# Scores of whole query rows for a pair of heads, moved from one 128x128 matmul form to four 64x64 quarters of the tensor engine

## The chip, the cores and the metric

The kernel runs on one core of one Trainium2 chip. The metric is device time in microseconds of one execution. A core has a matrix engine (TensorE, "PE" in the profile, with its weight loads "PEld"), a vector engine (VectorE, "DVE"), a scalar engine (ScalarE, "ACT"), a general engine (GpSimd, "POOL") and an engine that here only starts transfers ("SP").

## The reference

Block sparse attention in fp32, then two dense layers with a squared ReLU:

```python
batch, n_heads, seq, head_dim = (4, 8, 768, 64)   # blocks of 32 rows, 24 blocks
scores = scale * np.matmul(q, k.transpose(0, 1, 3, 2))
mask = np.abs(blk_i - blk_j) <= window            # window = 1
mask = mask | (blk_i == 0) | (blk_j == 0) | (blk_i == n_blocks - 1) | (blk_j == n_blocks - 1)
for qb in range(n_blocks):
    for kb in sampled_blocks[qb]:                 # 3 random blocks each
        mask[qb * block:(qb + 1) * block, kb * block:(kb + 1) * block] = True
scores = np.where(mask, scores, -1000000000.0)
scores = scores - np.max(scores, axis=-1, keepdims=True)
attn = np.exp(scores)
attn = attn / (np.sum(attn, axis=-1, keepdims=True) + 1e-09)
attn_out = np.matmul(attn, v)
...
x = attn_out.transpose(0, 2, 1, 3).reshape(B * S, H * D)     # 3072 x 512
h = np.maximum(x @ w_in, 0.0)                                # 512 -> 2048
return h * h @ w_out                                         # 2048 -> 512
```

The first and the last block of query rows look at all 768 keys. They are the "whole rows" of this case.

## The kernel before, in words

The 3072 rows are cut into 24 tiles of 128 (four batches of six), and these into eight chunks of three tiles. The dense layers run chunk by chunk: `turn` transposes a chunk's attention output (`xt`, `xh`, `xl`), `hidden` makes one of 16 pieces of the first layer (`ph`, 12 matmuls of 128x128 weights by 384 columns, in a rounded fp32 form as high and low parts), `project` adds a piece into the output (`po`, nine matmuls by 512 columns), and `split` makes the high and low parts of the weights (`wi`, `wo`; the low part is a subtraction on GpSimd). `gf`, `gh` and `gl` are the squared hidden values and their high and low parts.

Attention for a later chunk is cut into small steps and woven into the dense work of the chunk before by `Stream`: each unit is a generator that yields how many pieces of dense work pass before its next step (the table `LAG`). The order on each engine is therefore the order in which the program is written; each engine works through its list in that order and waits where an input is missing. There is a prologue without dense work, in which the attention of chunk 0 is made.

A unit of class `Half` is a tile's 128 query rows for four heads: scores `s` (matmuls of 64 rows of contraction by 32 query rows, in eight quarters of the array), maxima `m`, exponentials `p` or `pm`, and the product with the values `pv`.

A unit of class `Whole` is the first and last block of query rows for a pair of heads: 2 heads x 2 blocks x 32 = 128 rows. There are 16 of them: four batches by four pairs. Batch 0's run in the prologue, those of batches 1 to 3 are spread over some 48 us of dense work around the starts of chunks 1, 3 and 5. Its steps are `scores`, `maxima`, `exps`, `move` (copies on ScalarE and GpSimd into `pgm`), `turn_blocks` (a blockwise transpose on VectorE; in the prologue `turn` and `copies` with TensorE instead), `values` (`pvg`, 24 records for 12 matmuls of 128x64 weights) and `norm`. Scores and other results of TensorE share five PSUM banks by turns (`bank`).

`QG` holds the query rows of a unit as the stationary operand, 128 rows of contraction: 64 for the first head and 64 for the second. For a head's query columns the other head's 64 rows are zeros, written by the host:

```python
qg = np.zeros((B, 2, D, NPAIR, 2, 2, BLK), np.float32)
...
for e in range(2):
    qg[:, e, :, :, e] = q6[:, e]
```

`kn` holds the keys of two pairs, both heads of a pair on the two halves of the partitions. So one 128x128 matmul gives both heads' scores for 512 keys and a second for 256 keys; `load_whole` brings `QG` once a batch, 256 KB. The maxima are taken per row over both banks, and their larger one, times -SCALE, is the bias of the two exponentials.

Of the kernel before, what the change touches and what calls it, by code (L numbers as in the profile page):

```python
# [10 lines left out]
F32 = mybir.dt.float32  # L11
# [3 lines left out]
AF = mybir.ActivationFunctionType  # L15
ALU = mybir.AluOpType
AX = mybir.AxisListType.X
# [5 lines left out]
B, H, S, D = 4, 8, 768, 64  # L23
BLK = 32
NBLK = S // BLK
NRAND = 3
P = 128
NT = S // P
NJ = P // BLK
NPAIR = H // 2  # L30
# [4 lines left out]
SCALE = 0.125  # L35
# [61 lines left out]
def tile_block_sparse_attention_moe(ctx: ExitStack, tc, kd, knd, qd, qgd, vd, vnd, samp, const, wcat, out):  # L97
# [9 lines left out]
    nc = tc.nc  # L107
    wide = wcat.dtype != F32

    one = ctx.enter_context(tc.tile_pool(name="one", bufs=1))  # L110
    rot = ctx.enter_context(tc.tile_pool(name="rot", bufs=2, reuse_waits="tile"))
# [3 lines left out]
    def bank(name):  # L115
        return ps.tile([P, 512], F32, tag="s", name=name)
# [36 lines left out]
            )  # L153
        return idx

    QG = one.tile([P, NPAIR, P], F32, name="QG")
    V = {0: [one.tile([P, 2, NJ, HW // 2], F32, name=f"V{c}") for c in range(2)]}
    W1 = {f: one.tile([P, DM], F32, name=f"W1{f}") for f in SINGLE}
    KG = [one.tile([P, NJ, 2 + NRAND, NPAIR, BLK], F32, name=f"KG{i}") for i in range(2)]
# [8 lines left out]
    def load_whole(b, eng=nc.sync):  # L168

        eng.dma_start(QG.rearrange("p a b -> p (a b)"), qgd[b])  # L170

# [57 lines left out]
    def centre(qb):  # L229
        return min(max(qb, 1), NBLK - 2)  # L230
# [90 lines left out]
    class Half:  # L321
# [36 lines left out]
        def scores(self):  # L358
            b, t, u = self.b, self.t, self.u
            q, kg, kn = st["q", b, t], st["kg", b, t], st["kn", b, u]  # L360
            self.sb = [bank(f"s{self.name}_{e}") for e in range(2)]
            for i in range(2):
                pr = 2 * u + i
                for piece in range(2):
                    for g, j in enumerate(self.js):
                        c = centre(NJ * t + j)
                        for e in range(2):
                            r = slice(e * D, (e + 1) * D)
                            if piece == 0:
                                k, a, z = kn[r, c - 1 : c + 2, i, :], S_WIN, NSLOT  # L370
                            else:
                                k, a, z = kg[r, j, :, pr, :], 0, S_WIN
                            nc.tensor.matmul(  # L373
                                self.sb[e][g * BLK : (g + 1) * BLK, i * NSLOT + a : i * NSLOT + z],
                                q[r, j, pr, :],
                                k,
                                start=True,
                                stop=True,
                            )

        def maxima(self):
            m = self.m = rot.tile([P, 2, 2], F32, tag="m", name=f"m{self.name}", bufs=4)
            at = self.rows
            for e in range(2):
                nc.vector.tensor_reduce(  # L385
                    m[at, e], self.sb[e][at].rearrange("p (i c) -> p i c", i=2), axis=AX, op=ALU.max
                )
            self.p = rot.tile([P, 4, 2, NJ, BLK], F32, tag="p", name=f"p{self.name}", bufs=PBUFS)
            if not self.moved:
                nc.vector.tensor_scalar(m[at], m[at], -SCALE, None, op0=ALU.mult)  # L390
                return
            for e in range(2):
                nc.vector.tensor_tensor(  # L393
                    self.p[at, 2 * e : 2 * e + 2].rearrange("p h c a s -> p h (c a s)"),
                    self.sb[e][at].rearrange("p (i c) -> p i c", i=2),
                    m[at, e].unsqueeze(2).broadcast_to([at.stop, 2, NSLOT]),
                    op=ALU.subtract,
                )
# [29 lines left out]
        def exps(self):  # L428
            at = self.rows
            for e in range(2):  # L430
                for i in range(2):
                    nc.scalar.activation(  # L432
                        self.p[at, 2 * e + i].rearrange("p c a s -> p (c a s)"),
                        self.sb[e][at, i * NSLOT : (i + 1) * NSLOT],
                        AF.Exp,
                        scale=SCALE,
                        bias=self.m[at, e, i : i + 1],
                    )

        def turn(self, bank):  # L440
            pt = [bank(f"pt{self.name}_{e}") for e in range(2)]
            n = self.rows.stop
            for e in range(2):
                for i in range(2):
                    for c in range(2):
                        a = (2 * i + c) * P
                        nc.tensor.transpose(pt[e][:, a : a + n], self.p[:n, 2 * e + i, c], ident[:n, :n])
            return pt

        def copies(self, pt):  # L450
            self.pT = rot.tile([P, NJ, 4, 2, BLK], F32, tag="pT", name=f"pT{self.name}", bufs=2)
            n = len(self.js)
            for e in range(2):
                src = pt[e].rearrange("p (h j q) -> p h j q", h=4, j=NJ)[:, :, :n]
                dst = self.pT[:, :n, 2 * e : 2 * e + 2].rearrange("p j i c q -> p (i c) j q")
                if e == 0 or self.k < UC:
                    nc.scalar.copy(dst, src)  # L457
                else:
                    nc.vector.tensor_copy(dst, src)
# [63 lines left out]
    class Whole:  # L523


        n = (16 * BLK, 8 * BLK)

        def __init__(self, b, pr):
            self.b, self.pr = b, pr
# [24 lines left out]
            self.norm(po)  # L554

        def scores(self):
            b, pr = self.b, self.pr
            kn = st["kn", b, pr // 2]
            self.sg = [bank(f"g{self.name}_{i}") for i in range(2)]
            for i, n in enumerate(self.n):  # L560
                k0 = 16 * i
                nc.tensor.matmul(  # L562
                    self.sg[i][:, :n], QG[:, pr], kn[:, k0 : k0 + n // BLK, pr % 2, :], start=True, stop=True
                )

        def maxima(self):
            m = self.m = rot.tile([P, 2], F32, tag="mg", name=f"mg{self.name}", bufs=2)
            for i, n in enumerate(self.n):
                nc.vector.tensor_reduce(m[:, i : i + 1], self.sg[i][:, :n], axis=AX, op=ALU.max)
            nc.vector.tensor_tensor(m[:, 0:1], m[:, 0:1], m[:, 1:2], op=ALU.max)  # L570
            nc.vector.tensor_scalar(m[:, 0:1], m[:, 0:1], -SCALE, None, op0=ALU.mult)

        def exps(self):
            tag, bufs = ("w", WBUFS) if self.b > 0 else ("p", PBUFS)
            self.p = rot.tile([P, S], F32, tag=tag, name=f"pg{self.name}", bufs=bufs)
            for i, n in enumerate(self.n):
                at = slice(i * self.n[0], i * self.n[0] + n)
                nc.scalar.activation(self.p[:, at], self.sg[i][:, :n], AF.Exp, scale=SCALE, bias=self.m[:, 0:1])

        def move(self):  # L580

# [12 lines left out]

        def turn(self, bank):
            pt = [bank(f"ptg{self.name}_{i}") for i in range(2)]
            for i, n in enumerate(self.n):
                at = i * self.n[0]
                for a in range(0, n, P):
                    nc.tensor.transpose(pt[i][:, a : a + P], self.p[:, at + a : at + a + P], ident)  # L600
            return pt

        def copies(self, pt):
            self.pT = rot.tile([P, S], F32, tag="pT", name=f"pTg{self.name}", bufs=2)
            for i, n in enumerate(self.n):
                at = i * self.n[0]
                if i == 0:
                    nc.scalar.copy(self.pT[:, at : at + n], pt[i][:, :n])
                else:
                    nc.vector.tensor_copy(self.pT[:, at : at + n], pt[i][:, :n])  # L610

        def values(self, bank):
            b, pr = self.b, self.pr
            vn = st["vn", b, pr // 2]
            po = bank(f"pvg{self.name}")
            for kt in range(NT):
                for e in range(2):
                    h = pr % 2 * 2 + e
                    a = kt * P + e * D
                    nc.tensor.matmul(  # L620
                        po[e * D : (e + 1) * D, :VW],
                        self.pT[:, a : a + D],
                        vn[:, kt, h * VW : (h + 1) * VW],
                        start=(kt == 0),
                        stop=(kt == NT - 1),
                    )
            return po
# [270 lines left out]
    start = tc.tile_pool(name="start", bufs=1)  # L898
# [130 lines left out]
```

## Time and profile before

| | |
|---|---|
| time, median of 3 runs | 753.91 us (751.81 to 755.79) |
| span of the profiled execution | 752.7 us |
| around the span, against the median | 1.2 us |
| TensorE busy | 725.9 us, 96% |
| VectorE, ScalarE, GpSimd busy | 506.2, 518.8, 499.4 us |
| records of the whole rows' scores (L562) | 64, 16 units |

The profiled execution has no time of its own beside its span; the runs shown are others of the same kernel. Busy time of TensorE counts overlapping matmuls once. The profile shows a matmul's start as it was dispatched, and its end is modelled, so lengths of a group are read from the starts of what follows, not from its own busy time.

### The profile page before, as it was taken

The numbers are of one execution on the slowest core, as the hardware profiler recorded it, in microseconds if no ns is written. First come the engines' busy times: TensorE is split into PE (matmuls) and PEld (weight loads), VectorE is DVE, ScalarE is ACT, GpSimd is POOL, SyncE is SP. The second block draws the span as 40 slices with busy tenths as digits, with TensorE's granted clock in tenths as the row PEclk, the third lists the DMA queues.
The fourth block names the chain that finished last, engine by engine and source line by source line (L and its number), as shares of the span: only waits on it lengthen the run. The fifth ranks groups of instructions, "written<-read, shape, count | busy, mean of one in ns | idle before, by whom it ended". The sixth has DMA issues, their size and how long they took to land.

```text
span 752.7 us, 24232 instructions
## 1 busy us (share of the span) xinstructions
PE 725.9 (96%) x8936; PEld 606.6 (81%) x8936; DVE 506.2 (67%) x1036; ACT 518.8 (69%) x1145; POOL 499.4 (66%) x624
## 2 busy tenths in 40 slices
PE   5779999999999999999999999999999999999997
PEld 2566776678888888887888888888888888888986
DVE  5785876758785756677877675667878666555452
ACT  5986787888876875588786777478976776623222
POOL 6963644237786675757777567675776575777885
PEclk9989999999999999999999999999999999999999
DMA  8785889562533435533534435544344342101001
GB/s 276 222 237 141 234 246 348 144 163 62 145 83 97 136 83 176 150 96 97 139 90 102 131 85 166 152 101 129 89 119 108 82 130 57 34 1 43 1 1 42
DMA packets 85786, 92.95 MB, mean 123 GB/s; under 512 B 13539, under 2 KB 73060, under 8 KB 85668
## 3 DMA queue, kind: packets, MB, share of 16 engines
q1 hardware_dynamic: 79684, 68.42, 34.4%
q0 software_dynamic: 5696, 22.58, 9.1%
q8 instruction: 71, 1.16, 0.7%
q14 instruction: 47, 0.39, 0.2%
q10 hardware_dynamic: 288, 0.39, 0.1%
HBM read 85.05 MB, written 6.29 MB: 121 GB/s over the span
## 4 chain that ended last, share of the span: by engine, by line
PE 77%; ACT 12%; DVE 7%; issue 2%; DMA 1%; POOL 1%; ACTq 0%; DVEq 0%; POOLq 0%
PE ph L804 31%; PE po L842 29%; PE s L373 6%; PE pv L471 5%; PE po L832 2%; ACT p L432 2%; PE g L562 2%; PE pvg L620 1%; ACT pm L418 1%; DVE m L385 1%; ACT craw L726 1%; PE xt L789 1%; ACT V L217 1%; ACT r L808 1%; ACT pT L457 1%
## 5 line engine op out<-in xcount | busy, mean ns | idle before, releaser
L804 PE MATMUL ph<-xh,wi 128*128 128x384 f32 x832 | 237.8, 346 | 0.0
L418 ACT ACTIVATE pm<-p 32x256 f32<-32x256 f32 x528 | 219.2, 415 | 16.9 <-DVE p L393 9.4
L842 PE MATMUL po<-wo,gh 128*128 128x512 f32 x672 | 213.8, 399 | 0.0
L771 POOL TENSOR_TENSOR wi<-W,wi 128x512 fp32r<-128x512 f32 x104 | 143.0, 1375 | 73.3 <-DVE wi L770 37.6
L808 ACT ACTIVATE r<-ph 128x384 f32<-128x384 f32 x128 | 63.0, 492 | 172.5 <-PE ph L804 171.6
L771 POOL TENSOR_TENSOR wo<-WO,wo 128x512 fp32r<-128x512 f32 x112 | 146.2, 1305 | 50.0 <-DVE wo L770 44.2
L822 POOL TENSOR_TENSOR gl<-gf,gh 128x384 fp32r<-128x384 f32 x112 | 117.3, 1048 | 85.8 <-DVE gf L820 73.2
L804 PEld LDWEIGHTS ph<-xh,wi 128*128 128x128 f32 x832 | 150.3, 188 | 13.1 <-issue 7.2
L820 DVE SCALAR_TENSOR_TENSOR gf<-ph,r 128x384 f32<-128x384 f32 x112 | 62.3, 556 | 141.8 <-ACT r L808 129.2
L842 PEld LDWEIGHTS po<-wo,gh 128*128 128x128 f32 x672 | 123.5, 188 | 22.8 <-issue 2.8
L804 PE MATMUL ph<-xl,wi 128*128 128x384 f32 x416 | 141.4, 340 | 0.0
L842 PE MATMUL po<-wo,gl 128*128 128x512 f32 x336 | 133.3, 397 | 0.8 <-POOL gl L822 0.8
L804 PEld LDWEIGHTS ph<-xl,wi 128*128 128x128 f32 x416 | 78.2, 188 | 7.0 <-issue 2.9
L770 DVE CAST wo<-WO 128x512 fp32r<-128x512 f32 x112 | 83.1, 742 | 0.0
L842 PEld LDWEIGHTS po<-wo,gl 128*128 128x128 f32 x336 | 63.1, 188 | 17.0 <-POOL gl L822 2.3
L385 DVE TENSOR_REDUCE m<-s 128x2 f32<-128x512 f32 (+1 forms) x96 | 61.6, 682 | 9.3 <-PE s L373 8.9
L815 ACT ACTIVATE gh<-r 128x384 fp32r<-128x384 f32 x112 | 59.0, 527 | 9.3 <-POOL wo L771 0.4
L471 PEld LDWEIGHTS pv<-V,pT 128*32 128x32 f32 x2816 | 44.3, 111 | 22.5 <-issue 13.2
L471 PE MATMUL pv<-V,pT 128*32 128x65 f32 x2816 | 52.8, 224 | 7.8 <-ACT pT L457 3.1
L804 PE MATMUL ph<-xh,WI 128*128 128x384 f32 x192 | 54.3, 344 | 0.8 <-ACT xh L792 0.8
L373 PE MATMUL s<-KG,q 64*32 64x160 f32 x1408 | 49.2, 306 | 0.9 <-ACT KG L288 0.9
L393 DVE TENSOR_TENSOR p<-s,m 128x512 f32<-128x512 f32 (+1 forms) x72 | 46.0, 680 | 0.2
(90 smaller groups left out, 929.8 us busy)
## 6 DMA issues: line engine op xcount, KB each, us to landing
craw<-in_w_dram POOLq DMA_DIRECT2D x32, 512.0 KB, 6.3
V<-in_v_dram SPq DMA_DIRECT2D x462, 32.5 KB, 1.8
KG<-in_k_dram SPq DMA_DIRECT2D x198, 64.0 KB, 1.9
V<-in_v_dram SPq DMA_DIRECT2D x28, 390.0 KB, 4.4
q<-in_q_dram SPq DMA_DIRECT2D x24, 256.0 KB, 2.8
out_dram<-ot SPq DMA_DIRECT2D x22, 256.0 KB, 2.9
V<-in_v_dram SPq DMA_DIRECT2D x16, 292.5 KB, 4.7
vn<-in_vn_dram SPq DMA_DIRECT2D x5, 780.0 KB, 5.4
```

The lines of the kernel that those rows point to most:

```text
L373: nc.tensor.matmul(self.sb[e][g * BLK : (g + 1) * BLK, i * NSLOT + a : i * NSLOT + z], q[r, j, pr, :], k, start=True, stop=True,)
L385: nc.vector.tensor_reduce(m[at, e], self.sb[e][at].rearrange("p (i c) -> p i c", i=2), axis=AX, op=ALU.max)
L418: nc.scalar.activation(p[a * BLK : (a + 1) * BLK, g], x[g * BLK : (g + 1) * BLK, :, a], AF.Exp, scale=SCALE)
L471: nc.tensor.matmul(po[g * BLK : (g + 1) * BLK, h * VW : (h + 1) * VW], self.pT[:, src, 2 * e + i, c], v[:, self.u, j, hv : hv + VW], start ...
L770: nc.vector.tensor_copy(w[:, 0], src)
L771: nc.gpsimd.tensor_tensor(w[:, 1], src, w[:, 0], op=ALU.subtract)
L804: nc.tensor.matmul(ph[:, :TOK], w, x, start=(i == 0), stop=(i == len(steps) - 1))
L808: nc.scalar.activation(r, ph[:, :TOK], AF.Relu)
L815: nc.scalar.activation(gh, r, AF.Square)
L820: nc.vector.scalar_tensor_tensor(gf, ph[:, :TOK], 0.0, r, op0=ALU.max, op1=ALU.mult)
L822: nc.gpsimd.tensor_tensor(gl, gf, gh, op=ALU.subtract)
L842: nc.tensor.matmul(acc[c][u], g[:, at], w[:, k], start=(f == 0 and i == 0), stop=(f == NF - 1 and i == 2))
```

## The change

The contraction of 128 with its zeros goes. `QG` holds only 64 query columns a pair, each head's on its own half of the partitions (128 KB a batch). A unit's scores become four matmuls, each 64 rows of contraction by 64 query rows by 384 keys: by head `e` (row half of the array, and a bank of its own) and by half of the keys `kh` (column half of the array, and half of the bank's partitions). A bank now has one head: partitions 0 to 63 its 64 query rows against the first 384 keys, 64 to 127 the same rows against the other 384.

So a row's maximum is spread over two partition halves. Each half's maxima are scaled by -SCALE into the other half's place in `mo` (two TENSOR_SCALARs that cross the halves), and a SCALAR_TENSOR_TENSOR takes the smaller of the two negated ones into `mb`, the bias. The exponentials run over 384 columns twice instead of 512 and 256. `values` picks its 64 columns of `pTg` by head, key tile and half; the number and shape of its matmuls stay, as do those of `move`, `turn` and `copies`.

```diff
-    QG = one.tile([P, NPAIR, P], F32, name="QG")
+    QG = one.tile([P, NPAIR, D], F32, name="QG")
...
-            self.sg = [bank(f"g{self.name}_{i}") for i in range(2)]
-            for i, n in enumerate(self.n):
-                k0 = 16 * i
-                nc.tensor.matmul(
-                    self.sg[i][:, :n], QG[:, pr], kn[:, k0 : k0 + n // BLK, pr % 2, :], start=True, stop=True
-                )
+            self.sg = [bank(f"g{self.name}_{e}") for e in range(2)]
+            n = self.keys // BLK
+            for kh in range(2):
+                for e in range(2):
+                    r = slice(e * D, (e + 1) * D)
+                    nc.tensor.matmul(
+                        self.sg[e][kh * D : (kh + 1) * D, : self.keys],
+                        QG[r, pr],
+                        kn[r, kh * n : (kh + 1) * n, pr % 2, :],
+                        start=True,
+                        stop=True,
+                    )
...
-            for i, n in enumerate(self.n):
-                nc.vector.tensor_reduce(m[:, i : i + 1], self.sg[i][:, :n], axis=AX, op=ALU.max)
-            nc.vector.tensor_tensor(m[:, 0:1], m[:, 0:1], m[:, 1:2], op=ALU.max)
-            nc.vector.tensor_scalar(m[:, 0:1], m[:, 0:1], -SCALE, None, op0=ALU.mult)
+            for e in range(2):
+                nc.vector.tensor_reduce(m[:, e : e + 1], self.sg[e][:, : self.keys], axis=AX, op=ALU.max)
+            for kh in range(2):
+                at, of = (slice(x * D, (x + 1) * D) for x in (kh, 1 - kh))
+                nc.vector.tensor_scalar(o[at], m[of], -SCALE, None, op0=ALU.mult)
+            nc.vector.scalar_tensor_tensor(self.m, m, -SCALE, o, op0=ALU.mult, op1=ALU.min)
...
-            for i, n in enumerate(self.n):
-                at = slice(i * self.n[0], i * self.n[0] + n)
-                nc.scalar.activation(self.p[:, at], self.sg[i][:, :n], AF.Exp, scale=SCALE, bias=self.m[:, 0:1])
+            for e in range(2):
+                at = slice(e * self.keys, (e + 1) * self.keys)
+                nc.scalar.activation(
+                    self.p[:, at], self.sg[e][:, : self.keys], AF.Exp, scale=SCALE, bias=self.m[:, e : e + 1]
+                )
...
-                    a = kt * P + e * D
+                    a = (e * NT // 2 + k) * P + kh * D
```

No other instruction changes its place. On TensorE, the last unit of batch 1 stands in the middle of piece 5 of the first layer. Before (line, operation, result from inputs, size of the result):

```order
L804 MATMUL ph_5_3567<-xh_2968,wi_5_3339 128x384
L804 MATMUL ph_5_3567<-xl_2969,wi_5_3339 128x384
L804 MATMUL ph_5_3567<-xh_2968,wi_5_3339 128x384 x2
L562 MATMUL g_3_0_3575<-kn_1_2480,QG 128x512
L562 MATMUL g_3_1_3576<-kn_1_2480,QG 128x256
L804 MATMUL ph_5_3567<-xl_2969,wi_5_3339 128x384
L804 MATMUL ph_5_3567<-xh_2968,wi_5_3339 128x384 x2
```

And now, at the same place (`ph` of L804 is L820 in the changed file):

```order
L820 MATMUL ph_5_3602<-xl_2994,wi_5_3374 128x384
L820 MATMUL ph_5_3602<-xh_2993,wi_5_3374 128x384 x2
L566 MATMUL g_3_0_3610<-kn_1_2500,QG 64x384
L566 MATMUL g_3_1_3611<-kn_1_2500,QG 64x384
L566 MATMUL g_3_0_3610<-kn_1_2500,QG 64x384
L566 MATMUL g_3_1_3611<-kn_1_2500,QG 64x384
L820 MATMUL ph_5_3602<-xl_2994,wi_5_3374 128x384
L820 MATMUL ph_5_3602<-xh_2993,wi_5_3374 128x384 x2
```

Two instructions became four, with the same neighbours, and the second bank is written by the second instruction and not only after the whole of the first.

On VectorE, the maxima of the third unit of batch 2 stand between a `gf` and a weight's cast. Before:

```order
L820 SCALAR_TENSOR_TENSOR gf_2_6444<-ph_2_6421,r_2_6440 128x384
L569 TENSOR_REDUCE mg_2_6459<-g_2_0_6451 128x1
L569 TENSOR_REDUCE mg_2_6459<-g_2_1_6452 128x1
L570 TENSOR_TENSOR mg_2_6459<-mg_2_6459 128x1
L571 TENSOR_SCALAR mg_2_6459<-mg_2_6459 128x1
L770 CAST wo_3_6472<-WO_1394 128x512
```

Now:

```order
L836 SCALAR_TENSOR_TENSOR gf_2_6494<-ph_2_6471,r_2_6490 128x384
L580 TENSOR_REDUCE mg_2_6511<-g_2_0_6501 128x1
L580 TENSOR_REDUCE mg_2_6511<-g_2_1_6502 128x1
L583 TENSOR_SCALAR mo_2_6512<-mg_2_6511 64x2 x2
L584 SCALAR_TENSOR_TENSOR mb_2_6513<-mg_2_6511,mo_2_6512 128x2
L786 CAST wo_3_6527<-WO_1414 128x512
```

Four operations became five, and what stands behind them waits for one more.

More of the change, by code (lines that the diff above doesn't have):

```diff
@@ L523, in tile_block_sparse_attention_moe @@
     class Whole:
-        n = (16 * BLK, 8 * BLK)
+        keys = S // 2
+        parts = (16 * BLK, 8 * BLK)
         def __init__(self, b, pr):
@@ L558, in scores @@
             kn = st["kn", b, pr // 2]
-            self.sg = [bank(f"g{self.name}_{i}") for i in range(2)]
-            for i, n in enumerate(self.n):
-                k0 = 16 * i
-                nc.tensor.matmul(
-                    self.sg[i][:, :n], QG[:, pr], kn[:, k0 : k0 + n // BLK, pr % 2, :], start=True, stop=True
-                )
-        def maxima(self):
-            m = self.m = rot.tile([P, 2], F32, tag="mg", name=f"mg{self.name}", bufs=2)
-            for i, n in enumerate(self.n):
-                nc.vector.tensor_reduce(m[:, i : i + 1], self.sg[i][:, :n], axis=AX, op=ALU.max)
-            nc.vector.tensor_tensor(m[:, 0:1], m[:, 0:1], m[:, 1:2], op=ALU.max)
-            nc.vector.tensor_scalar(m[:, 0:1], m[:, 0:1], -SCALE, None, op0=ALU.mult)
+            self.sg = [bank(f"g{self.name}_{e}") for e in range(2)]
[10 more added lines that the diff above has]
+                    )
+        def maxima(self):
+            m = rot.tile([P, 2], F32, tag="mg", name=f"mg{self.name}", bufs=2)
+            o = rot.tile([P, 2], F32, tag="mo", name=f"mo{self.name}", bufs=2)
+            self.m = rot.tile([P, 2], F32, tag="mb", name=f"mb{self.name}", bufs=2)
+            for e in range(2):
[4 more added lines that the diff above has]
+            nc.vector.scalar_tensor_tensor(self.m, m, -SCALE, o, op0=ALU.mult, op1=ALU.min)
         def exps(self):
@@ L596, in turn @@
             pt = [bank(f"ptg{self.name}_{i}") for i in range(2)]
-            for i, n in enumerate(self.n):
-                at = i * self.n[0]
+            for i, n in enumerate(self.parts):
+                at = i * self.parts[0]
                 for a in range(0, n, P):
@@ L604, in copies @@
             self.pT = rot.tile([P, S], F32, tag="pT", name=f"pTg{self.name}", bufs=2)
-            for i, n in enumerate(self.n):
-                at = i * self.n[0]
+            for i, n in enumerate(self.parts):
+                at = i * self.parts[0]
                 if i == 0:
@@ L616, in values @@
             for kt in range(NT):
+                kh, k = divmod(kt, NT // 2)
                 for e in range(2):
                     h = pr % 2 * 2 + e
-                    a = kt * P + e * D
+                    a = (e * NT // 2 + k) * P + kh * D
                     nc.tensor.matmul(
@@ L988 @@
     vn = np.concatenate([vb[:, V_STATIC : V_STATIC + 1], vb[:, 1 : NBLK - 1], vb[:, V_STATIC + 1 :]], axis=1)
-    qg = np.zeros((B, 2, D, NPAIR, 2, 2, BLK), np.float32)
-    q6 = pairs(q).reshape(B, 2, D, NBLK, NPAIR, BLK)[:, :, :, [0, NBLK - 1]].transpose(0, 1, 2, 4, 3, 5)
-    for e in range(2):
-        qg[:, e, :, :, e] = q6[:, e]
+    qg = pairs(q).reshape(B, P, NBLK, NPAIR, BLK)[:, :, [0, NBLK - 1]].transpose(0, 1, 3, 2, 4)
     kp = pairs(k)
@@ L1002 @@
         "in_q_dram": pairs(q),
-        "in_qg_dram": qg.reshape(B, P, NPAIR * P),
+        "in_qg_dram": np.ascontiguousarray(qg).reshape(B, P, NPAIR * D),
         "in_v_dram": vb.reshape(B, NVB * BLK, HW),
```

## The prediction

> **What bounds the kernel now.** I read the page's busy shares and clock first, then the groups by form, the stretches, the chain of waits, and last single instructions in order of time.
>
> ```profile
> PE 725.9 (96%) x8936; PEld 606.6 (81%) x8936; DVE 506.2 (67%) x1036; ACT 518.8 (69%) x1145; POOL 499.4 (66%) x624
> PEclk9989999999999999999999999999999999999999
> PE 77%; ACT 12%; DVE 7%; issue 2%; DMA 1%; POOL 1%; ACTq 0%; DVEq 0%; POOLq 0%
> L562 PE MATMUL g<-kn,QG 128*128 128x512 f32 x32 | 18.0, 644 | 6.8 <-DMA kn<-in_kn_dram 6.8
> L562 PE MATMUL g<-kn,QG 128*128 128x256 f32 x32 | 10.0, 395 | 0.0
> ```
>
> TensorE is the bound (96% busy, 77% of the chain), its clock practically full. The line that changes, L562, holds 28 us of it: 64 records for 32 instructions, so an fp32 product goes through in two passes. Where is a microsecond of TensorE worth a microsecond? Busy time by stretch (columns: stretch, length, then PE, PEld, DVE, ACT, POOL busy, clock, DMA):
>
> ```profile
> 137.00:326.00 189.00, 188.76 (x2348) 157.33 (x2347) 130.70 (x269) 141.69 (x322) 120.29 (x121) 1.00 0.44 117
> 326.00:355.40 29.40, 28.76 (x263) 24.09 (x261) 21.84 (x49) 25.24 (x59) 19.44 (x27) 1.00 0.43 118
> 355.40:500.50 145.10, 145.09 (x1954) 125.48 (x1955) 101.16 (x203) 102.85 (x238) 101.08 (x95) 1.00 0.44 119
> 500.50:530.20 29.70, 28.79 (x264) 24.10 (x262) 21.84 (x49) 25.26 (x59) 19.45 (x28) 1.00 0.42 115
> ```
>
> From 137 us on, TensorE is full, except in two spells of some 30 us (326 to 355.4 and 500.5 to 530.2) with 0.6 and 0.9 us idle. There the chain leaves TensorE and comes back to it through other engines (chain, then that matmul in order of time):
>
> ```profile
> 325.99 0.50 ACT r L808
> 352.24 1.17 DVE mg L570
> 354.34 1.02 POOL gl L822
> 355.40 0.49 PE L842 MATMUL po<-wo,gl 128*128 128x512 f32 x1 [0.39 <-POOL gl L822]
> ```
>
> So in the spells a faster TensorE only waits longer, and a slower VectorE or GpSimd is paid for. Twelve of the sixteen units (pairs of heads) run after 137 us: eight outside the spells, four inside (332.7, 347.9, 507.2, 522.7 us).
>
> **The scores' matmuls.** A unit in steady work:
>
> ```profile
> 189.38 0.51 PE L804 MATMUL ph<-xh,wi 128*128 128x384 f32 x2
> 189.73 1.45 PE L562 MATMUL g<-kn,QG 128*128 128x512 f32 x4
> 191.19 0.34 PE L804 MATMUL ph<-xh,wi 128*128 128x384 f32 x1
> ```
>
> The two ph before it start 0.17 apart (189.38 to 189.73), so that is what a 384-column ph takes. One ph lies between g and 191.19, so the unit takes 191.19 - 0.17 - 189.73 = 1.29 us: 2 x 768 columns at 0.84 ns. Nothing is lost at its ends, since the array keeps its one shape.
>
> The new unit has four matmuls of 64x64 x 384 columns in two passes. The trace has no 64*64 form; the nearest are 128*64 (pvg) and 64*32 (s):
>
> ```profile
> 178.66 0.34 PE L804 MATMUL ph<-xl,wi 128*128 128x384 f32 x1
> 178.92 0.92 PE L620 MATMUL pvg<-vn,pTg 128*64 128x65 f32 x24
> 179.77 0.62 PE L804 MATMUL ph<-xh,wi 128*128 128x384 f32 x2
> 180.23 0.33 PE L804 MATMUL ph<-xl,wi 128*128 128x384 f32 x1
> 182.37 0.48 PE L373 MATMUL s<-KG,q 64*32 64x160 f32 x16
> 182.65 0.37 PE L373 MATMUL s<-kn,q 64*32 64x96 f32 x16
> ```
>
> The s rows: 16 records of 160 columns in 0.28 us (182.37 to 182.65). At 0.84 ns a column that is two rounds of eight at once: two row halves and four column quarters run side by side, each with keys of its own. So four quarters should too: two passes of 384 x 0.84 = 0.32, 0.64 us. The pvg rows give the price of a change of shape: the ph before ends at 178.66 + 0.17 = 178.83, and the two after it are followed by one at 180.23, so they begin in effect at 179.89. That is 1.06 us for 12 steps of 65 columns (0.66 us by 0.84 ns): some 0.38 us (1.06 less 0.66, and a little for starting each step) go to the two changes of shape, in and out. New unit: 0.64 + 0.38 = 1.02 us, a gain of 0.27. Bounds: 0.64 with a free change (gain 0.65), 0.38 + 4 x 0.64 = 2.94 if nothing overlaps (loss 1.65). I take 1.02, since both terms come from rows of the same fp32 work in quartered shapes.
>
> The Trainium skill (TensorEngine Tiling (Array Packing), Overview, Theoretical Speedup) promises up to 2x for each small dimension; by that alone a unit would take 0.64 us, the rival below. Its Tiling Modes section says that a change of mode drains the engine; the 0.38 us of the pvg rows agree.
>
> The first unit of the twelve follows a tiled pv at 141.7 and pays about half the switch already before: gain 0.27 + 0.2 = 0.47. ScalarE, on the chain just after it, had only this to give:
>
> ```profile
> 144.66 0.49 ACT L808 ACTIVATE r<-ph 128x384 f32<-128x384 f32 x1 [0.39 <-PE ph L804]
> ```
>
> So 0.4. Outside the spells: 0.4 + 7 x 0.27 = **2.3 us**. Inside: nothing, as POOL gl ends the wait there.
>
> **The maxima.** Two reductions of 512 and 256 columns become two of 384, and so do the two exponentials: the same elements, no change. Then a TENSOR_TENSOR (L570) and a TENSOR_SCALAR (L571) become two TENSOR_SCALARs of 64x2 and a SCALAR_TENSOR_TENSOR of 128x2. Durations are min/median/max in ns:
>
> ```profile
> L570 DVE TENSOR_TENSOR mg<-mg x16: 159/576/1306, 10.2 to 541.1; 128x1 f32<-128x1 f32 x16
> L571 DVE TENSOR_SCALAR mg<-mg x16: 153/154/155, 10.4 to 542.4; 128x1 f32<-128x1 f32 x16
> 352.09 1.28 POOL L771 TENSOR_TENSOR wo<-WO,wo 128x512 fp32r<-128x512 f32 x1
> 352.24 1.15 DVE L570 TENSOR_TENSOR mg<-mg 128x1 f32<-128x1 f32 x1
> 353.42 0.15 DVE L571 TENSOR_SCALAR mg<-mg 128x1 f32<-128x1 f32 x1
> 353.44 0.34 POOL L587 COPY pgm<-pg 32x192 f32<-32x192 f32 x1
> 25.36 0.40 POOL L217 COPY V<-vn 32x260 f32<-32x260 f32 x1
> 25.54 0.25 DVE L390 TENSOR_SCALAR m<-m 96x4 f32<-96x4 f32 x1
> ```
>
> Undisturbed, one more dependent operation is 0.2 us a unit (10.18 to 10.38 in the chain below). But L570, with two SBUF inputs, lasts until GpSimd's running operation ends (353.39 against 353.37), while L571, one element a partition, never does. L390, four elements a partition, did: it ends at 25.79, GpSimd's copy at 25.76. The new 64x2 operations have two elements, so they too may be held: three such operations a unit instead of one. The Trainium skill gives the reason: VectorE: DVE Perf Modes (What auto-detection actually checks) lets an even count in SBUF take the two-port mode, and Advanced Engine Details and Errata (GPSIMD Details) has the Pool engine share an interface with such operations and with two-input ones; the three rows agree.
>
> Mostly this costs nothing: VectorE idles about 30% between 137 and 326 us. In the spells three maxima stand on the chain (351.3, 510.0, 526.1 us). There I charge 0.2 us each, **0.6 us**: when the first is held to the end of a GpSimd operation, the others follow close to its next, a short copy (353.44). Bounds: 0 (an end held by GpSimd is the same end), to two further waits of a 1.28 us split for each of three units, 7.7 us.
>
> **The prologue.** Its chain:
>
> ```profile
> 1.34 5.37 DMA kn<-in_kn_dram
> 6.75 2.94 PE g L562 x4
> 9.72 0.44 DVE mg L569
> 10.18 0.17 DVE mg L570
> 10.38 0.16 DVE mg L571
> 10.56 1.05 ACT pg L578 x2
> 45.12 0.65 PE L471 MATMUL pv<-V,pT 128*32 128x65 f32 x11 [1.21 <-issue]
> ```
>
> Here a column takes 1.9 ns (2.94 us for 1536). Two passes of 384 side by side end about 1.5 us after 6.75, and two reductions of some 0.55 us and three small operations (0.2 each) put ScalarE's start near 10.2 instead of 10.56. QG's transfer is halved (256 to 128 KB), which may land kn a little sooner. Later waits that none of this moves (1.2 us at 45 us, behind something the profile doesn't show) may eat it: 0 to 0.6, I take **0.3 us**. The other three QG transfers are issued a chunk early; that is hidden behind TensorE's work. The new order of pT's columns in the values changes addresses, not counts.
>
> **Sum** against this execution's own span: 752.7 - 2.3 + 0.6 - 0.3 = 750.7. The median of the runs shown, 753.91, stands 1.2 above the span, so I predict 751.9 us, 0.3% less. About 0.5% (3.8 us) is what a measurement of this kernel can tell from no change.
>
> **The rivals.**
> 1. The change of shape is free (a 64*64 drain overlaps its neighbours). Gain 0.65 x 7 + 0.8 = 5.4 outside the spells, less 0.3 net of the other terms: 753.9 - 5.1 = 748.8. Against it: the 0.38 us of pvg. Chance 0.15.
> 2. The two key halves share their rows and stream one after the other: unit 0.38 + 1.29 = 1.67, a loss of 0.38 x 7 + 0.2 = 2.9, with the other terms 757.1. Against it: the s rows, where four column quarters share rows. Chance 0.07; all four in a row 0.03 (unit 2.94: 13.0 us outside the spells, 4 x 1.65 less 1.5 of idle inside, 772 us).
> 3. On the other side: VectorE's three held operations take turns with GpSimd's 1.28 us splits in the spells. The gain of 2.6 us (2.3 + 0.3) is used up when the six added waits (two in each of three units) average 0.43 us; at 1.07 us the kernel is 0.5% slower, at the full 1.28 it takes 753.9 - 2.6 + 7.7 = 759.0. For it: the 1306 ns of L570. Against it: GpSimd's next operation at 353.44 was a short copy. Chance 0.13, 0.10 of it over 0.5%.
> 4. The forecast: 0.62, its own range 750.4 to 753.4.
>
> Faster by over 0.5% (below 750.1): rival 1 and a little of the forecast, 0.18. Slower (above 757.7): 0.10 of rival 3 and the serial case, 0.13. The rest, 0.69, lies within. Range: half a microsecond beyond rivals 1 and 2, to 748.3 and 757.2; outside are rival 3's upper part, the serial case and a tail of rival 1, 0.17.
>
> **What would show it.** Right: L562's successor as 128 records of form 64*64, four starting within some 30 ns, the next full-array matmul's effective start 1.0 us after the last one's end; the first spell's ACT r some 1.8 us earlier than 325.99 (0.4 + 4 x 0.27 + 0.3), TensorE's idle time in each spell up by 0.5 to 0.9. Wrong: starts 0.32 us apart within a pass (rival 2), a gap-free change (rival 1), or 64x2 operations lasting over 0.5 us and longer waits for POOL gl at the spells' ends (rival 3). What would upset the sum most is a spell whose end moves by more than a microsecond, either way: a bank that is freed later, or a different interleaving of VectorE and GpSimd.

## The result, and the profile after

The changed kernel takes 749.5 us (median of 6 runs, 748.09 to 751.04) beside 754.09 us of the kernel before on the same chip: ratio 0.9939, 95% interval 0.9916 to 0.9961. That is 0.6% or 4.6 us less; 751.9 us and 0.3% less were forecast, with a range of 748.3 to 757.2 us. From the page of the changed kernel, the busy shares and the engines of the chain, and then the group of the new line:

```profile
PE 717.3 (96%) x9000; PEld 596.6 (80%) x9000; DVE 509.1 (68%) x1052; ACT 518.5 (69%) x1145; POOL 497.0 (67%) x624
PE 79%; ACT 8%; DMA 4%; DVE 3%; POOL 2%; issue 2%; SPq 1%; ACTq 0%; POOLq 0%; DVEq 0%
L566 PE MATMUL g<-kn,QG 64*64 64x384 f32 x128 | 15.8, 574 | 6.3 <-DMA kn<-in_kn_dram 6.3
```

TensorE is still the bound, and 8.6 us less busy. (That is not the gain: kernels with the instructions of the kernel before read 723.1 to 725.9 us in their profiles.) The 64 records of form 128*128 became 128 of form 64*64. The same unit as in the prediction, in order of time, with its first and its second pass apart (x4 is four records, merged):

```profile
186.97 0.34 PE L820 MATMUL ph<-xh,wi 128*128 128x384 f32 x1
187.24 0.55 PE L566 MATMUL g<-kn,QG 64*64 64x384 f32 x4
...
187.61 0.50 PE L566 MATMUL g<-kn,QG 64*64 64x384 f32 x4
188.05 0.45 PE L820 MATMUL ph<-xl,wi 128*128 128x384 f32 x1
188.33 0.34 PE L820 MATMUL ph<-xh,wi 128*128 128x384 f32 x1
```

All four quarters start within the first pass, 0.02 us from the first start to the fourth, and again within the second. The last ph before them ends at 186.97 + 0.17 = 187.14; the one behind them is followed by another at 188.33, so it begins in effect at 188.16. The unit takes 1.02 us, where 1.02 was forecast and 1.29 stood before; the nine other units that lie between full-array matmuls agree to 0.01 us. The passes stand 0.37 apart (0.32 would be 384 columns at 0.84 ns), and the rest, some 0.33, lies at the two ends.

To see where the time went I cut the work at places that both kernels have: the first unit in dense work, the start of the ACT r that opens each spell, and the PE matmul whose wait for POOL gl closes it. The granted clock was 1.00 in all of them. Busy time by these stretches (columns as in the prediction), before:

```profile
141.68:325.99 184.31, 184.07 (x2293) 154.43 (x2287) 127.08 (x263) 137.78 (x314) 119.47 (x121) 1.00 0.44 117
325.99:355.40 29.41, 28.77 (x263) 24.09 (x261) 21.84 (x49) 25.25 (x59) 19.44 (x27) 1.00 0.43 118
355.40:500.49 145.09, 145.09 (x1954) 125.48 (x1955) 101.16 (x203) 102.84 (x238) 101.08 (x95) 1.00 0.44 119
500.49:530.19 29.70, 28.79 (x264) 24.09 (x262) 21.84 (x49) 25.26 (x59) 19.45 (x27) 1.00 0.42 115
```

And after:

```profile
140.08:322.18 182.10, 181.77 (x2313) 151.50 (x2307) 128.33 (x268) 137.60 (x314) 119.18 (x121) 1.00 0.44 118
322.18:351.66 29.48, 28.19 (x271) 22.83 (x269) 22.07 (x51) 25.27 (x59) 19.45 (x27) 1.00 0.44 117
351.66:495.55 143.89, 143.89 (x1962) 124.28 (x1963) 101.88 (x205) 102.83 (x236) 100.70 (x95) 1.00 0.45 118
495.55:525.29 29.74, 28.16 (x271) 22.84 (x269) 22.05 (x51) 25.25 (x59) 19.43 (x27) 1.00 0.44 116
```

The spells kept their length (29.41 to 29.48, 29.70 to 29.74), and TensorE's idle time in them grew from 0.64 to 1.29 and from 0.91 to 1.58 us. Both are what the prediction said. But the full stretches lost 2.21 us (five units, 1.48 forecast) and 1.20 us (two units, 0.54 forecast). Behind the second spell, from its end to the start of the last 15 matmuls of the second layer, 214.27 us became 213.04 (744.46 less 530.19, 738.33 less 525.29): 1.23 us less with one unit in it, 0.27 forecast. All three are too much by nearly the same 0.7 to 1.0 us, which the number of units does not explain. The rest of the difference of the two spans, 1.6 us, lies before the first unit (141.68 to 140.08). Not all of that can be put down to the edit: up to 137 us the granted clock was 0.96 in the profile before and 0.99 in this one. The ACT r that opens the first spell came 3.81 us earlier (1.60 before the first unit, 2.21 behind it), where 1.8 was forecast.

What changed there shows where no unit and no attention stands, in the chain of both kernels (piece, length, count). Before:

```profile
404.57 2.08 PE ph L804 x12
406.65 2.10 PE po L842 x9
408.75 2.08 PE ph L804 x12
410.83 2.10 PE po L842 x9
```

After:

```profile
400.44 2.08 PE ph L820 x12
402.52 2.06 PE po L858 x9
404.58 2.08 PE ph L820 x12
406.67 2.06 PE po L858 x9
```

Nine matmuls of the second layer take 2.06 us instead of 2.10, though no line of theirs was touched. Over 200 to 745 us, the mean distance from one record's start to the next of its kind, without the pairs that have something else or a missing record between them (the pitch), is 232.8 ns before and 229.8 after for the second layer, 173.7 and 174.4 for the first. With 1008 and some 1344 such matmuls that is 3.0 us less and 0.9 more: 2.1 us, by this estimate, that the sum did not have.

### The profile page after: what moved, and what is told of

It is laid out like the page before. It is cut to its first block, busy times and chain, and to the rows that moved or that the text cites. A ratio compares the mean times of both kernels' runs of the same rounds, so it can differ in the third digit from the quotient of the medians.

```text
span 746.6 us, 24386 instructions
## 1 busy us (share of the span) xinstructions
PE 717.3 (96%) x9000; PEld 596.6 (80%) x9000; DVE 509.1 (68%) x1052; ACT 518.5 (69%) x1145; POOL 497.0 (67%) x624
## 4 chain that ended last, share of the span: by engine, by line
PE 79%; ACT 8%; DMA 4%; DVE 3%; POOL 2%; issue 2%; SPq 1%; ACTq 0%; POOLq 0%; DVEq 0%
PE ph L820 32%; PE po L858 29%; PE s L373 6%; PE pv L471 5%; PE po L848 3%; DMA V<-in_v_dram 2%; ACT pm L418 2%; PE pvg L636 1%; ACT V L217 1%; DMA KG<-in_k_dram 1%; PE g L566 1%; PE xt L805 1%; ACT pg L591 1%; PE pt L447 1%; SPq L314 1%
## 5 line engine op out<-in xcount | busy, mean ns | idle before, releaser
L820 PE MATMUL ph<-xh,wi 128*128 128x384 f32 x832 | 238.1, 347 | 0.0
L858 PE MATMUL po<-wo,gh 128*128 128x512 f32 x672 | 211.5, 396 | 0.0
L787 POOL TENSOR_TENSOR wo<-WO,wo 128x512 fp32r<-128x512 f32 x112 | 144.7, 1292 | 50.1 <-DVE wo L786 42.1
L820 PEld LDWEIGHTS ph<-xh,wi 128*128 128x128 f32 x832 | 150.6, 188 | 13.1 <-issue 6.2
L820 PE MATMUL ph<-xl,wi 128*128 128x384 f32 x416 | 141.2, 339 | 0.0
L820 PEld LDWEIGHTS ph<-xl,wi 128*128 128x128 f32 x416 | 78.1, 188 | 10.0 <-issue 6.5
L820 PE MATMUL ph<-xh,WI 128*128 128x384 f32 x192 | 54.1, 342 | 0.8 <-ACT xh L808 0.8
```

What stands on the lines that cost most here:

```text
L787: nc.gpsimd.tensor_tensor(w[:, 1], src, w[:, 0], op=ALU.subtract)
L820: nc.tensor.matmul(ph[:, :TOK], w, x, start=(i == 0), stop=(i == len(steps) - 1))
L858: nc.tensor.matmul(acc[c][u], g[:, at], w[:, k], start=(f == 0 and i == 0), stop=(f == NF - 1 and i == 2))
```

## The experiments

**Where the tiles lie.** The smaller `QG` (1 KB a partition less) moves all later tiles 1024 bytes down. The new small tiles `mo` and `mb` take four times 32 bytes, so the tiles allocated after them (the attention's `p`, `pT` and `x`, most of `WO`, and `xh`, `xl`, `r`, `gh`, `gf`, `gl`) lie 128 bytes further from the weight buffers (`wi`, `wo`) than before. Three kernels take this apart. The first puts everything back in its old place:

```diff
-    QG = one.tile([P, NPAIR, D], F32, name="QG")
+    QG = one.tile([P, 2 * NPAIR * D], F32, name="QG")[:, : NPAIR * D].rearrange("p (a b) -> p a b", b=D)
...
-            m = rot.tile([P, 2], F32, tag="mg", name=f"mg{self.name}", bufs=2)
-            o = rot.tile([P, 2], F32, tag="mo", name=f"mo{self.name}", bufs=2)
-            self.m = rot.tile([P, 2], F32, tag="mb", name=f"mb{self.name}", bufs=2)
+            mg = rot.tile([P, 6], F32, tag="mg", name=f"mg{self.name}", bufs=2)
+            m, o, self.m = mg[:, 0:2], mg[:, 2:4], mg[:, 4:6]
```

> The changed kernel with every tile at its address of the kernel before (QG padded back to 2 KB a partition, the three small maxima tiles in one 32-byte slot). Theory A (about half of the gain comes from where the tiles lie in SBUF: the second layer's matmuls by 512 columns start 232.8 ns apart before and 229.8 ns after): the pitch goes back to about 233 ns, the time to about 0.3% below the kernel before, 751.8 us or a ratio of 0.997. Theory B (the pitch comes from which of the seven weight buffers a weight is put into, which also differs): the pitch stays near 230 ns and the ratio near 0.994. Theory C (the shape alone, by chip or run): the same as B.

Measured: 750.59 us, ratio 0.9965 (0.9952 to 0.9978). The pitch of the second layer is 232.8 ns again, that of the first 173.9. Its stretches:

```profile
142.44:325.28 182.84, 182.47 (x2312) 151.47 (x2307) 128.28 (x268) 137.64 (x313) 119.47 (x121) 1.00 0.44 117
325.28:354.75 29.47, 28.29 (x272) 22.82 (x270) 22.05 (x51) 25.25 (x59) 19.45 (x27) 1.00 0.45 117
354.75:499.27 144.52, 144.52 (x1962) 124.28 (x1963) 101.62 (x205) 102.86 (x237) 100.90 (x95) 1.00 0.44 118
499.27:529.01 29.74, 28.28 (x271) 22.82 (x269) 22.05 (x51) 25.24 (x59) 19.43 (x27) 1.00 0.43 116
```

This is the change without its move of the tiles, and behind the first unit it is the sum of the prediction: 1.47 us less in the first stretch (1.48 forecast), 0.57 in the third (0.54), 0.17 behind the second spell (529.01 to 743.11; 0.27 forecast), and the spells 0.06 and 0.04 longer.

The second kernel keeps the small `QG` and merges only the small tiles (all later tiles move by 1024 bytes, none against another); the third keeps `QG` at its old size and the three tiles apart (only the 128 bytes).

> The changed kernel with its QG of 1 KB, but the three small maxima tiles in one slot: all tiles behind QG are 1024 bytes lower than before, and the dense layers' tiles have their old distance to the weight buffers. Theory A1 (the shift of 1024 counts): pitch 230 ns, ratio 0.994. Theory A2 (the distance of 128 bytes between weights and hidden values counts): pitch 233 ns, ratio 0.997.

> The changed kernel with QG padded to 2 KB but three small maxima tiles: weight buffers at their old addresses, the hidden values and inputs of the dense layers 128 bytes higher. Theory A1: pitch 233 ns, ratio 0.997. Theory A2: pitch 230 ns, ratio 0.994.

Measured: 750.44 us, 0.9958 (0.9942 to 0.9974), pitches 232.8 and 173.7 for the first of them; 750.05 us, 0.9946 (0.9926 to 0.9966), pitches 230.5 and 175.1 for the second. So the 128 bytes change the pitch, and the 1024 do not. The three times alone are too close to be told apart; the pitches decide. But with the same 128 bytes the pitches are not the changed kernel's 229.8 and 174.4: from the first unit to the last 15 matmuls of the second layer the second kernel of these two takes 599.75 us (143.11 to 742.86), the changed one 598.25 (140.08 to 738.33), and the one with the old places 600.67 (142.44 to 743.11).

**The same move without the change.** If so, the kernel before must gain from it. First only `gh`, `gl` and `gf` are moved, by a wider `r` ahead of them:

```diff
-        r = pool["x"].tile([P, TOK], F32, tag="r", name=f"r{c}_{f}", bufs=2)
+        r = pool["x"].tile([P, TOK + 16], F32, tag="r", name=f"r{c}_{f}", bufs=2)[:, :TOK]
```

> The kernel before, old matmul shape, with only the squared hidden values (gh, gl, gf) 128 bytes higher in SBUF, by a gap behind r; weights and xh, xl stay. Theory (the distance between the second layer's stationary gh, gl and its weights sets that layer's pitch): 512-column pitch near 230.3 ns instead of 232.8, the first layer's 384-column pitch unchanged at 173.7, so 1008 x 2.4 ns = 2.4 us faster from the second half on, ratio 0.997. Rival (the gain belongs to the changed form or to xh, xl): pitch 232.8, ratio 1.000.

Measured: 752.57 us, 0.9986 (0.9971 to 1.0000), pitches 232.1 and 173.7: by the pitch, a quarter of the effect. So the distance of `gh` and `gl` from the weights `wo`, with which they go into the second layer's matmuls, is not the whole of it. Then all tiles behind the maxima's, by a wider `mg` (24, 40 and 72 columns for 128, 256 and 512 bytes):

```diff
-            m = self.m = rot.tile([P, 2], F32, tag="mg", name=f"mg{self.name}", bufs=2)
+            m = self.m = rot.tile([P, 24], F32, tag="mg", name=f"mg{self.name}", bufs=2)
```

> The kernel before, computation and order untouched; only the tile of the maxima (mg) is wider, so that every tile allocated after it (the dense inputs, r, gh, gl, gf and WO among them) lies 128 bytes further from the weight buffers, as in the changed kernel. Placement theory: the pitch of the second layer's matmuls falls from 232.8 to about 230 ns, that of the first layer rises from 173.7 to about 175, and the time falls by 0.15 to 0.3% (1.0 to 2.2 us), though no score, maximum or exponential changed. Moving gh, gl and gf alone had brought only 232.1 ns, so the partner must lie among the other late tiles. Rival (the pitch follows the new form of the units, not the placement): pitch 232.8 and the time of the kernel before within 0.1%.

> The same with 256 bytes instead of 128 (mg wider still). If the pitch depends on where the late tiles lie within a short repeating pattern of addresses, it comes out anywhere between 229 and 234 ns for the second layer, and 256 need not continue what 128 did; if more distance is simply better, the second layer falls below 230 ns. Time: 1008 and 1344 matmuls times the changes of the two pitches, within 0.1%.

> The same with 512 bytes. A pattern that repeats within 512 bytes gives the pitches of the kernel before back (232.8 and 173.7 ns) and its time; otherwise the pitches differ again, and the time by 1008 and 1344 matmuls times their changes, within 0.1%.

| kernel before, late tiles moved by | second layer, ns | first layer, ns | time, us | ratio |
|---|---|---|---|---|
| 0 | 232.8 | 173.7 | 753.86 | 1 |
| 128 bytes | 229.9 | 174.5 | 752.29 | 0.9980 (0.9964 to 0.9995) |
| 256 bytes | 232.8 | 173.7 | 753.71 | 1.0011 (0.9990 to 1.0032) |
| 512 bytes | 232.8 | 173.7 | 754.01 | 1.0010 (0.9991 to 1.0028) |

(The ratios, with their 95% intervals, are estimated from the single runs and are not quotients of the medians beside them.) The effect comes at 128 and is gone at 256 and at 512 bytes, as it would if it repeated every 256; other distances were not tried. In the chain the pieces that took 2.10 us before take, with 128 bytes:

```profile
404.07 2.08 PE ph L804 x12
406.15 2.06 PE po L842 x9
```

And with 256:

```profile
403.27 2.08 PE ph L804 x12
405.35 2.10 PE po L842 x9
```

The stretches of the kernel with 128 bytes:

```profile
142.12:325.71 183.59, 183.32 (x2293) 154.50 (x2287) 127.22 (x263) 137.67 (x313) 118.92 (x121) 1.00 0.44 117
325.71:355.12 29.41, 28.76 (x263) 24.19 (x261) 21.83 (x49) 25.25 (x59) 19.38 (x27) 1.00 0.44 119
355.12:499.52 144.40, 144.40 (x1954) 125.49 (x1955) 100.35 (x203) 102.74 (x237) 100.65 (x95) 1.00 0.45 119
499.52:529.21 29.69, 28.81 (x263) 24.22 (x261) 21.84 (x49) 25.25 (x59) 19.36 (x27) 1.00 0.43 116
```

Less than before by 0.72 us in the first, 0.69 in the third, and 0.95 behind the second spell (529.21 to 742.53); the spells are unmoved, since POOL gl ends them. So the two effects add up, stretch by stretch (us against the kernel before):

| stretch | scores alone | 128 bytes alone | their sum | the change |
|---|---|---|---|---|
| first unit to first spell | -1.47 | -0.72 | -2.19 | -2.21 |
| first spell | +0.06 | 0.00 | +0.06 | +0.07 |
| between the spells | -0.57 | -0.69 | -1.26 | -1.20 |
| second spell | +0.04 | -0.01 | +0.03 | +0.04 |
| to the last 15 of the second layer | -0.17 | -0.95 | -1.12 | -1.23 |
| all | -2.11 | -2.37 | -4.48 | -4.53 |

**The maxima alone.** The kernel before, with the three new small operations, as in the change, in place of its two (its scores and exponentials stay). The small tiles share one slot, so that no other tile moves:

```diff
-            m = self.m = rot.tile([P, 2], F32, tag="mg", name=f"mg{self.name}", bufs=2)
+            mg = rot.tile([P, 6], F32, tag="mg", name=f"mg{self.name}", bufs=2)
+            m, o, self.m = mg[:, 0:2], mg[:, 2:4], mg[:, 4:6]
...
```

> The kernel before with only the new small operations: two 64x2 TENSOR_SCALARs across the partition halves and a SCALAR_TENSOR_TENSOR in place of TENSOR_TENSOR and TENSOR_SCALAR (the bias is then a mix of two rows' maxima, which a softmax cancels). It tests the term of 0.6 us. Forecast: 0.6 us slower, the ends of the two spells 0.2 and 0.4 us later. Rival (a held operation ends with GpSimd's anyway): 0 to 0.1 us. Rival (three operations take turns with GpSimd's splits): 2 us or more slower, 64x2 operations of over 0.5 us more than once in a unit.

Its bias pairs the halves of the partitions as the changed kernel's does, while the scores are laid out as before; the division by the sum takes the bias out again. Measured: 754.07 beside 753.89 us, ratio 1.0001 (0.9987 to 1.0015), and the waits at the ends of the spells, 0.39 and 0.38 before, are:

```profile
354.97 0.50 PE L845 MATMUL po<-wo,gl 128*128 128x512 f32 x1 [0.46 <-POOL gl L825]
...
529.84 0.49 PE L845 MATMUL po<-wo,gl 128*128 128x512 f32 x1 [0.46 <-POOL gl L825]
```

That is 0.07 and 0.08 us a spell. Why so little shows at the end of the first spell of the changed kernel, on VectorE and then in the chain, which here runs through GpSimd alone:

```profile
348.42 1.35 DVE L583 TENSOR_SCALAR mo<-mg 64x2 f32<-64x2 f32 x2
349.81 0.18 DVE L584 SCALAR_TENSOR_TENSOR mb<-mg,mo 128x2 f32<-128x2 f32 x1
```

```profile
348.29 1.28 POOL wo L787
349.66 0.32 POOL pgm L602
350.01 0.53 POOL pgm L602
350.61 1.01 POOL gl L838
```

The first 64x2 operation is held to the end of GpSimd's split, as L570 was; the second and the SCALAR_TENSOR_TENSOR run at 0.16 to 0.18 us beside the first of GpSimd's copies. Between the split and gl GpSimd has only these two copies, which are of an earlier unit and do not wait for the new maxima. What grew is the second copy, which took in the kernel before:

```profile
353.81 0.46 POOL pgm L587
```

In the kernel with the maxima alone this copy takes 0.53 and 0.52 us in the two spells: that is what the wait grew by, to 0.01 us. Over the whole kernel (min/median/max in ns) at most one operation of a unit is held for long, the first:

```profile
L583 DVE TENSOR_SCALAR mo<-mg x32: 161/164/1212, 9.0 to 536.3; 64x2 f32<-64x2 f32 x32
L584 DVE SCALAR_TENSOR_TENSOR mb<-mg,mo x16: 160/160/219, 9.4 to 537.5; 128x2 f32<-128x2 f32 x16
```

**The prologue.** ScalarE's first exponential was forecast near 10.2 instead of 10.56. After:

```profile
9.60 1.28 ACT L591 ACT_TABLE_LOAD   x1 [9.60 <-DVE mb L584]
10.89 1.05 ACT L591 ACTIVATE pg<-g,mb 128x384 f32<-128x384 f32 x2
```

The bias was ready by 9.51, earlier than forecast, in part because kn landed at 6.27 instead of 6.71 us (VectorE's operation for the bias):

```profile
9.35 0.16 DVE L584 SCALAR_TENSOR_TENSOR mb<-mg,mo 128x2 f32<-128x2 f32 x1
```

But the load of ScalarE's tables, which stood at 0.75 us before, now stands behind the wait for that bias and takes 1.28 us on the chain. Before:

```profile
0.75 1.28 ACT L578 ACT_TABLE_LOAD   x1 [0.75 <-PEq L1020]
```

The chain after has a step of ScalarE's sequencer at L591 just ahead of the load (9.55 us), the chain before has none there. The kernels with the old scores and exponentials load at 0.74 to 0.75 us, `maxima_alone` too; the three above with the new ones at 9.67 to 9.80. The next kernel asks for an exponential of one column at the very start, so that the load goes there:

```diff
-    below = one.tile([P, 1], F32, name="below")
+    below = one.tile([P, 2], F32, name="below")
+    below, warm = below[:, 0:1], below[:, 1:2]
     nc.gpsimd.memset(below, 2.0**-14 - 0.5)
+    nc.scalar.activation(warm, below, AF.Exp)
```

> The changed kernel with one exponential of a single column ahead of everything on ScalarE, so that the load of its function table (1.28 us) no longer waits for the first maxima, behind which it stands since the change (9.60 us instead of 0.75). All tiles lie as in the changed kernel. Theory (the prologue's start on ScalarE is on the path): the first unit's exponentials start at 9.6 us instead of 10.9, and the time falls by 0.5 to 1.3 us against the changed kernel, ratio to before 0.992. Rival (later waits of the prologue absorb it): exponentials start as early, the time stays, ratio 0.994.

```profile
0.75 1.28 ACT L125 ACT_TABLE_LOAD   x1 [0.75 <-PEq L1035]
...
9.60 1.05 ACT L593 ACTIVATE pg<-g,mb 128x384 f32<-128x384 f32 x2 [7.35 <-DVE mb L586]
```

The exponentials start 1.29 us sooner. The time is 748.15 us, ratio 0.9933 (0.9914 to 0.9951); the changed kernel had 0.9939, so a microsecond is not excluded and not shown. Nor are the two kernels alike behind the prologue: the first unit starts at 138.30 instead of 140.08 us, but from there to the last 15 matmuls of the second layer it is 599.55 us (to 737.85) instead of 598.25, with pitches of 230.5 and 175.2 ns instead of 229.8 and 174.4. The two programs put every operand of these matmuls at the same address, so the place of the tiles is not all that sets the pitch. The last of the family puts the small tiles together, widens `r` (as above) and loads the tables early:

> The changed kernel with the early table load, the three small maxima tiles in one slot (so that xh and xl keep their old distance to the weights) and gh, gl, gf 128 bytes higher. Theory: 512-column pitch 230 ns or less, 384-column pitch 173.7 instead of the changed kernel's 174.4, so another 1344 x 0.7 ns = 0.9 us beside what the table load brings: 748 us, ratio 0.991. Rival (the first layer's pitch rises with gh too): 384-column pitch 174.4 or more, ratio 0.993.

Measured: 748.22 us, 0.9928 (0.9911 to 0.9946); pitches 232.0 and 173.7, as with the wider `r` on the kernel before. Both beat the kernel before; neither is told apart from the changed one.

Last, the new form with its old places, but batch 0's four units (all of the prologue's) in the old form:

```diff
+            if b == 0:
+                for i, n in enumerate(self.parts):
+                    nc.tensor.matmul(
+                        self.sg[i][:, :n],
+                        QG0[:, pr],
+                        kn[:, 16 * i : 16 * i + n // BLK, pr % 2, :],
+                        start=True,
+                        stop=True,
+                    )
+                return
...
```

> The changed form for batches 1 to 3 only; the four units of the prologue have the old matmuls, maxima and QG layout, and all tiles lie as in the kernel before. Against the same places with the new form everywhere (ratio 0.9965) it shows the prologue's term. Forecast as it was (the new form saves 0.3 us there): 0.3 us slower than that, ratio 0.997. With the table load that waits in the new form (1.28 us later, 0.4 to 0.5 us net): 0 to 0.5 us faster than that, ratio 0.996.

Measured: 752.2 us, 0.9976 (0.9958 to 0.9994), beside 0.9965 (0.9952 to 0.9978) with the new form in the prologue too. The new form there is worth 0.8 us by the two ratios, with intervals that overlap. A single profile can't settle it: the first unit after the prologue starts at 141.68 us before, at 140.50 with 256 bytes and at 138.87 with 512, in three kernels whose prologues have the same instructions. The granted clock up to 137 us was 0.96, 1.00 and 1.00 in these profiles, so the clock alone does not explain it.

## Why the prediction was right, point by point

- **The bound, and where time counts: right.** TensorE's full stretches gave the gain, the spells gave nothing, their idle time rose by 0.65 and 0.67 us (0.5 to 0.9 forecast). The waits for POOL gl and ACT pg took it up (us in total, times, longest; from 137 to 745 us). Before:

```profile
PE s L373 <- ACT pg L578: 0.8, 2, 0.5
PE po L842 <- POOL gl L822: 0.8, 2, 0.4
```

After:

```profile
PE po L858 <- POOL gl L838: 1.5, 2, 0.8
PE s L373 <- ACT pg L591: 1.3, 2, 0.8
```

- **The scores' matmuls: right.** 1.02 us a unit, and 2.21 us (1.47 + 0.57 + 0.17) in place of 2.3 outside the spells when the tiles keep their places. Rival 1 (a free change of shape) and rival 2 (halves in turn) fall with the rows of the unit. The Trainium skill (TensorEngine Tiling (Array Packing), Overview, Theoretical Speedup) says "Up to 2×" for a dimension of at most 64. Here a unit went from 1.29 to 1.02 us: two passes of 0.32 would be half of 1.29, and the rest is what the row of pvg had priced.
- **The maxima: right in kind, too large.** 0.6 us forecast, about 0.15 measured (0.07 and 0.08 in the two spells). The failed step is that each of the three maxima in the spells adds 0.2 us to the chain. The chain there runs through GpSimd's split, its two copies and gl, and none of these waits for the operations behind the held one; the wait for POOL gl grew by less than one of them, by what the second copy took longer. Rival 3 (held operations taking turns) falls: one operation of a unit is held for long, not three. Its sign is there by the letter, 64x2 operations of up to 1.21 us and a wait for POOL gl that went from 0.4 to 0.8 us; but that wait grew because TensorE came earlier, and the spells kept their length.
- **The prologue: the step failed, the term can't be told.** ScalarE started at 10.89, not 10.2, because the forecast did not count the table load, which until then had stood at 0.75. The work ahead of it was faster than forecast (the bias at 9.51). What the new form is worth there, 0.8 us by two ratios that overlap, agrees with the 0.3 forecast and with nothing at all.
- **What the sum lacked: 2.4 us.** It took every instruction that the change doesn't touch at its old duration. The tiles' addresses moved, and with them the pitch of 1008 matmuls. So 749.5 lies near rival 1's 748.8, but not by its mechanism: a unit that takes 0.64 us is refuted, and the difference to the forecast of 2.4 us (751.9 to 749.5) is the size of what the 128 bytes give to the kernel before. The forecast's own range, 750.4 to 753.4, was missed; with the tiles in their old places the time, 750.59 us, lies in it. That 749.5 is still within the stated range is luck, since the range reached so far down for rival 1 alone.
- **Arithmetic.** Half a microsecond beyond rival 2's 757.1 is 757.6, not the 757.2 of the range; nothing here hangs on it.

What stays open is why the pitch follows the place. The move of `gh`, `gl` and `gf` alone does little, so one of the other tiles that moved (`p`, `pT`, `x`, `xh`, `xl`, `r`, `WO`) has part in it; this was not taken further apart. Open too is what makes the pitches of two kernels with the same 128 bytes 0.7 ns longer than in the changed kernel (230.5 and 175.1, 230.5 and 175.2); with one profile of each, a property of the kernel can't be told from one of that execution.

## What to carry to other kernels

Price a change of the array's shape by a row of the same kernel that pays it already (here pvg's 0.38 us a unit, in and out); in this one case the forecast from it held to some hundredths of a microsecond. Before a small operation is charged to a chain, ask what stands between it and the wait that ends last: here it was another engine's own list. When a change alters the size of any tile, compare the start-to-start distance of matmuls that it doesn't touch, before a difference is put down to the edit; a control kernel with the old addresses separates the two. Look also for what a first instruction of its kind pulls along: here a table load of 1.28 us moved from ahead of a wait to behind it.

## What was not expected of the hardware

The pitch of a dense fp32 matmul stream differs with the place of tiles in SBUF: 232.8 against 229.9 ns for 512 columns and 173.7 against 174.5 for 384 when tiles are moved by 128 bytes, with not one instruction different, and the old pitches again at 256 and 512 bytes. The Trainium skill (SBUF — State Buffer, SBUF: two separate sides) says of the engines' side that "only the shared port pair causes contention" and that TensorE never waits there. By that alone the pitch would not follow the place of a tile; it does here, by 1.2% for 512 columns. The measurement decides that it does, and not why.

The four quarters do run side by side in fp32: four starts within 0.02 us in one pass, the second pass 0.37 us after the first, for 384 columns.
